# A fused attention and mixture-of-experts kernel: token halves and eight placing transfers, unused rows zeroed by VectorE, a reordered start and two changes at the gates

## The chip, the cores and the metric

The kernel runs on one NeuronCore of a Trainium2 chip. The metric is the device time of one execution in microseconds, from three runs, of which the median counts. The engines are named as the profile names them: PE is TensorE (matmul; PEld its weight load), DVE is VectorE, ACT is ScalarE, POOL is GpSimd, SP is SyncE, which only issues DMA transfers; ACTq is the queue of transfers that ACT issues.

## What is computed

Four batches of eight heads of masked attention over 768 tokens of 64 numbers, and then a layer of eight experts of which each token takes its two best. A pair of tokens is masked out unless q and k have the same nearest of 16 centroids.

```python
q_assign = np.argmax(np.einsum('bhsd,hcd->bhsc', q_n, c_n), axis=-1)
k_assign = np.argmax(np.einsum('bhsd,hcd->bhsc', k_n, c_n), axis=-1)
mask = q_assign[:, :, :, None] == k_assign[:, :, None, :]
scores = np.where(mask, scale * np.matmul(q, k.transpose(0, 1, 3, 2)), -1e9)
attn = softmax(scores); x = attn @ v            # x: 3072 tokens of 512
noisy_logits = x @ w_gate + np.log1p(np.exp(x @ w_noise)) * noise
# the two best of 8 experts per token, softmax of their two logits as weights
out[mask] += top2_w[mask, k, None] * (np.maximum(x[mask] @ w1[e], 0.0) @ w2[e])
```

## The kernel before

**Attention** runs over 16 pairs of heads, p = 0 to 15, twelve steps to a pair (two heads s of six key chunks kc). A step computes the scores of 128 keys against all 768 queries (`scores`, L540 to L549: two matmuls per half of the queries, one of A and one of B, and exp on ACT), `split_p` takes the low part of the result on POOL (L560), and four steps later `values` multiplies with v (L581 to L587). A and B are operands of 128 rows: the high and low parts of q and k, the cluster mask in rows 64 to 80 of A, the negated maxima in rows 96 and 97 of B. Three of each exist and take turns (p % 3); rows that nothing writes are zeroed, and two rows of ones set, once for each of the three by `fixed_init` (L344 to L346).

**The preparation of a pair** comes some steps ahead: `a_split` transposes q and k (L414, PE), copies the high part (L423, ACT) and subtracts for the low part (L424, DVE), into the tile hl (xt for p = 1); `b_place` moves these by DMA into A and B (L488); `a_sims` and `a_sum` (L435, L450) give the similarities with the centroids; five operations on DVE make one-hot rows of them, the mask chain (L454, L458, L462, L467, L471); `a_mask` transposes these (L480) and copies them (L482, ACT, tile mk), `b_mask` moves them into A. `b_max` computes the plain q times k in high parts (L517) and reduces it to row maxima (L520, DVE, 24 reductions per pair), `b_neg` (L527 to L529) and `b_negT` (L534, L536, a DMA) put the negated maxima into B. For p = 0 the last three run for each head alone, before its scores.

**The order** is written out by hand: `attention` (from L200) gives each piece of work a place `at(step, function)` in steps and thirds of steps, from the table AT and some formulas; negative places run before the first score. Each engine executes its instructions in the order in which the code then writes them, waiting for what they need. SP's and ACT's transfers are issued in order as well. PSUM results go to a ring of six banks (`ps()`), and one further bank, aux, is shared by half of the maxima of `b_max` and the gate's small results.

**The gate** (`g_gate`) runs once per batch, three times among the steps and the last time in the experts' beginning, as a list of small pieces that `chain` and `emit` write out. Its `places` multiplies the chosen experts with a triangle and with ones (L780, L784) to count each token's place in its expert's list; L799 and L801 read the counts; L812, L813, L817, L818 and L827 (DVE) and L814 (ACT) pack the results for the lists.

**The experts** go through tokens in tiles: layer 1 (L1271), layer 2 (L1309). w2 is split into high (L1155, ACT) and low parts (L1157, DVE), four quarters, by `split_w2(e, c)`; `eff` issues layer 2 of a tile. For the first expert the quarters are split between pieces of the last gate.

Of the kernel before, what the change touches and what calls it, by code (L numbers as in the profile page):

```python
# [34 lines left out]
    vd=[1, 1, 2, 3, 4, 5], sec=-6.0, qf=-4.0, place1=0.0,  # L35
    fv=[{'v': -5.0, 'vscale': 13.0, 'am': 24.333, 'amstep': 0.333, 'vsplit': 25.333, 'vstep': 2.0},
        {'v': 9.0, 'vscale': 11.667, 'am': 13.333, 'amstep': 0.333, 'vsplit': 15.0, 'vstep': 1.667}],
# [7 lines left out]
class Kernel:  # L45
# [154 lines left out]
    def attention(self, ctx):  # L200
# [6 lines left out]
        self.fix = fix = ctx.enter_context(tc.tile_pool(name="fix", bufs=1))  # L207
        self.A = [fix.tile([128, 2, 2, S], F32R, name=f"A{i}") for i in range(3)]
        self.Bt = [fix.tile([128, 2, 2, S], F32R, name=f"B{i}") for i in range(3)]
        self.oh = [fix.tile([128, 2, 3, 4, 32], BF, name=f"oh{i}") for i in range(2)]  # L210
# [17 lines left out]
        for p in range(NP):  # L228
# [178 lines left out]
    def a_split(self, p, i, s):  # L407

        nc = self.nc
        b, hp = divmod(p, self.H // 2)  # L410
        qk = self.qk[b, hp // 2]
        t = self.ps()[:, :384]
        for m in range(3):
            nc.tensor.transpose(t[:, m * 128:m * 128 + 128],  # L414
                                qk[:, i, 2 * (hp % 2) + s, 2 * m:2 * m + 2, :].rearrange("p j d -> p (j d)"),
                                self.ident)
        if (i, s) == (0, 0):

# [3 lines left out]
        hi, lo = hl[:, 1 + i, s], hl[:, 3 - 3 * i, s]  # L422
        nc.scalar.activation(hi, t, AF.Copy)  # L423
        nc.vector.tensor_tensor(lo, t, hi, op=OP.subtract)  # L424

    def a_sims(self, p, s):

        nc, st = self.nc, self.st[p]
        hp = p % (self.H // 2)
        t = self.ps()[:, :384]  # L430
        n = 0
        for i in range(2):
            c0 = 64 - 64 * i
# [68 lines left out]
    def b_mask(self, p):
        mk, A = self.st[p]["mk"], self.A[p % 3]
        for i in range(2):
            for a in range(2):
                self.dma(A[64:80, i, :, 384 * a:384 * a + 384], mk[64 * i + 32 * a:64 * i + 32 * a + 16],
                         self.nc.scalar if p < 3 and a else None)

    def b_max(self, p, s, j):

        nc, st, A = self.nc, self.st[p], self.A[p % 3]
        if (s, j) == (0, 0):
            st["mm"] = self.wk.tile([128, 2 * self.NJ], F32, name="mm")
        c = self.NJ * s + j
        for n in range(2):
            t = self.ps()[:, :384]
            nc.tensor.matmul(t, A[:, 0, s, j * 128:j * 128 + 128],  # L517
                             A[:, 1, s, n * 384:n * 384 + 384], start=True, stop=True)
            o = st["mm"][:, c:c + 1] if n else self.aux[:, 500 + c:501 + c]
            nc.vector.tensor_reduce(o, t, axis=X, op=OP.max, negate=True)  # L520

    def b_neg(self, p, s, n):

        v, W, c = self.nc.vector, n * self.NJ, self.NJ * s
        o = self.aux[:, 500 + c:500 + c + W]
        hi, lo = (self.nm[:, W * i:W * i + W] for i in range(2))
        v.tensor_tensor(o, o, self.st[p]["mm"][:, c:c + W], op=OP.min)  # L527
        v.tensor_copy(hi, o)
        v.tensor_tensor(lo, o, hi, op=OP.subtract)  # L529

    def b_negT(self, p, s, n):
# [4 lines left out]
        nc.scalar.activation(nt[:W], t[:W, :128], AF.Copy)  # L536
        self.dma(self.Bt[p % 3][96:98, 1, s:s + n], nt[:W], nc.scalar if p < 2 else None)


    def scores(self, p, s, kc):  # L540
        nc, st, A, Bt = self.nc, self.st[p], self.A[p % 3], self.Bt[p % 3]
        ks = slice(kc * 128, kc * 128 + 128)
        pe = self.wk.tile([128, 2, 384], F32, name="pe", bufs=6)
        for n in range(2):
            t = self.ps()[:, :384]
            ns = slice(n * 384, n * 384 + 384)
            for M, qi in ((A, 0), (Bt, 1)):
                nc.tensor.matmul(t, M[:, 1 - qi, s, ks], M[:, qi, s, ns], start=not qi, stop=bool(qi))  # L548
            nc.scalar.activation(pe[:, n], t, AF.Exp, bias=self.l64[:, 0:1], scale=self.scale)  # L549
# [168 lines left out]
    def g_gate(self, b):  # L718
# [183 lines left out]
    def experts(self, ctx):  # L902
# [31 lines left out]
        for f in range(NF):  # L934
# [434 lines left out]
```

## Time and profile before

| | |
|---|---|
| three runs | 1053.3, 1053.99, 1056.56 us; median 1053.99 |
| the profiled execution | 1051.78 us, span 1050.0 us from the first to the last instruction |
| PE busy | 993.1 us, 95% of the span |
| DVE, POOL, ACT busy | 662.6, 575.7, 509.5 us |
| mean granted clock of PE | 0.987 of full speed |

All rows below come from the one profiled execution. An engine's order of time lists start, duration, line and operation, out<-in and the count of alike ones in a row, and in brackets how long the engine had been idle and what released it. "Busy" of a stretch is the sum for each engine in it, in the order PE, PEld, DVE, ACT, POOL, and then come PEclk, the share of the DMA engines and GB/s; PEclk is the clock granted to PE as a share of full speed (1.00 is 2.4 GHz, 0.50 is 1.2 GHz).

### The profile page before, as it was taken

The numbers are of one execution on the slowest core, as the hardware profiler recorded it, in microseconds if no ns is written. First come the engines' busy times: TensorE is split into PE (matmuls) and PEld (weight loads), VectorE is DVE, ScalarE is ACT, GpSimd is POOL, SyncE is SP. The second block draws the span as 40 slices with busy tenths as digits, with TensorE's granted clock in tenths as the row PEclk, the third lists the DMA queues.
The fourth block names the chain that finished last, engine by engine and source line by source line (L and its number), as shares of the span: only waits on it lengthen the run. The fifth ranks groups of instructions, "written<-read, shape, count | busy, mean of one in ns | idle before, by whom it ended". The sixth has DMA issues, their size and how long they took to land.

```text
span 1050.0 us, 21873 instructions
## 1 busy us (share of the span) xinstructions
PE 993.1 (95%) x8353; PEld 672.8 (64%) x8353; DVE 662.6 (63%) x1443; ACT 509.5 (49%) x1059; POOL 575.7 (55%) x631
## 2 busy tenths in 40 slices
PE   5789999999999999899999999999999999999994
PEld 4678998988888888784555545455454454554541
DVE  4787777787778777996646556545555455445421
ACT  3468776767686767577243416234153151421510
POOL 9168786868997799882355225242252442523211
PEclk9699999999999999999999999999999999999997
DMA  7866978787878766317396928729259297391201
GB/s 190 210 168 137 223 175 208 172 202 165 209 181 194 172 148 148 125 53 172 112 210 167 218 95 190 188 85 250 92 143 220 74 189 179 105 235 69 61 34 35
DMA packets 172879, 162.79 MB, mean 155 GB/s; under 512 B 87737, under 2 KB 151609, under 8 KB 172770
## 3 DMA queue, kind: packets, MB, share of 16 engines
q1 hardware_dynamic: 159132, 124.65, 50.6%
q0 software_dynamic: 13296, 36.38, 12.3%
q8 instruction: 67, 1.10, 0.4%
q10 hardware_dynamic: 342, 0.32, 0.2%
q14 instruction: 42, 0.34, 0.1%
HBM read 78.21 MB, written 26.51 MB: 100 GB/s over the span
## 4 chain that ended last, share of the span: by engine, by line
PE 41%; issue 7%; POOL 2%; DMA 2%; ACT 1%; DVE 1%; SPq 0%; POOLq 0%; ACTq 0%
PE ring L1271 20%; PE ring L1309 18%; POOL out L1321 1%; PE ring L1299 1%; DMA xT<-xg 1%; POOL xt L1284 1%; PE ring L1302 0%; PE ring L1176 0%; DMA xg<-xs,idx 0%; DMA xs<-xh 0%; PE ring L692 0%; POOL xh L652 0%; SPq L1262 0%; DMA out<-yo,idx 0%; PE ring L700 0%
## 5 line engine op out<-in xcount | busy, mean ns | idle before, releaser
L560 POOL TENSOR_TENSOR pl<-pe 128x768 f16<-128x768 f32 x173 | 252.0, 1471 | 63.1 <-ACT pe L549 51.7
L1271 PE MATMUL ring<-xT,w1t 128*128 128x416 f16 (+2 forms) x1536 | 272.8, 339 | 0.5 <-DMA xT<-xg 0.5
L1309 PE MATMUL ring<-w2t,hT 128*128 128x512 f16 x1152 | 252.5, 379 | 0.6 <-ACT w2t L1155 0.5
L549 ACT ACTIVATE pe<-ring,l 128x384 f32<-128x384 f32 x384 | 201.1, 578 | 66.9 <-PE ring L548 61.6
L1271 PEld LDWEIGHTS <-w1t 128*128 128x128 f16 x1536 | 149.3, 98 | 119.2 <-issue 1.6
L1309 PEld LDWEIGHTS <-hT 128*128 128x128 f16 x1152 | 112.1, 98 | 134.2 <-issue 1.5
L1148 ACT ACTIVATE hr<-ring 128x416 f32<-128x416 f32 (+2 forms) x128 | 66.5, 519 | 271.1 <-PE ring L1271 271.1
L1321 POOL DMA_INDIRECT out<-yo,idx x52 | 62.3, 1199 | 223.5 <-DVE yo L1317 109.9
L520 DVE TENSOR_REDUCE aux<-ring 128x1 f32<-128x384 f32 x192 | 107.8, 562 | 65.0 <-PE ring L517 56.5
L548 PE MATMUL ring<-A 128*128 128x384 f32 x384 | 143.2, 373 | 1.7 <-ACT mk L482 0.7
L548 PE MATMUL ring<-B 128*128 128x384 f32 x384 | 129.5, 337 | 0.0
L1151 DVE TENSOR_TENSOR hT<-hr,hT 128x416 f16<-128x416 f32 (+3 forms) x128 | 70.6, 557 | 81.5 <-ACT hT L1150 81.3
L517 PE MATMUL ring<-A 128*128 128x384 f32 x384 | 109.2, 359 | 10.3 <-ACT pe L549 3.4
L1317 DVE SCALAR_TENSOR_TENSOR yo<-ring,we,xt 128x512 f32<-128x512 f32 (+1 forms) x49 | 36.7, 748 | 121.0 <-PE ring L1309 106.9
L520 DVE TENSOR_REDUCE mm<-ring 128x1 f32<-128x384 f32 x192 | 105.0, 547 | 0.5 <-PE ring L517 0.5
L1251 POOL DMA_INDIRECT xg<-xs,idx x52 | 57.3, 1102 | 83.1 <-DMA xT<-xg 73.5
L581 PE MATMUL av<-vv,pe 128*128 128x65 f16 x1152 | 97.1, 195 | 0.4 <-DVE stg L595 0.2
L583 PE MATMUL av<-vv,pe 128*128 128x64 f16 x1152 | 96.2, 192 | 0.0
L581 PEld LDWEIGHTS <-pe 128*128 128x128 bf16 x1152 | 79.4, 99 | 15.2 <-issue 10.2
L517 PEld LDWEIGHTS ring<-A 128*128 128x128 f32 x384 | 71.3, 193 | 23.0 <-ACT pe L549 12.5
L583 PEld LDWEIGHTS <-pe 128*128 128x128 bf16 x1152 | 77.8, 98 | 0.3
L548 PEld LDWEIGHTS ring<-A 128*128 128x128 f32 x384 | 73.1, 190 | 6.5 <-ACT pe L549 2.0
(224 smaller groups left out, 1383.3 us busy)
## 6 DMA issues: line engine op xcount, KB each, us to landing
stg<-in_moe_w SPq DMA_DIRECT2D x64, 512.0 KB
A<-hl SPq DMA_DIRECT2D x30, 384.0 KB
B<-hl SPq DMA_DIRECT2D x30, 384.0 KB
vt<-in_v SPq DMA_DIRECT2D x8, 768.0 KB
out<-zt SPq DMA_DIRECT2D x12, 512.0 KB
A<-hl SPq DMA_DIRECT2D x60, 96.0 KB
B<-hl SPq DMA_DIRECT2D x30, 192.0 KB
xs<-xh SPq DMA_DIRECT2D x15, 384.0 KB
```

The source lines that it names most:

```text
L517: nc.tensor.matmul(t, A[:, 0, s, j * 128:j * 128 + 128], A[:, 1, s, n * 384:n * 384 + 384], start=True, stop=True)
L520: nc.vector.tensor_reduce(o, t, axis=X, op=OP.max, negate=True)
L548: nc.tensor.matmul(t, M[:, 1 - qi, s, ks], M[:, qi, s, ns], start=not qi, stop=bool(qi))
L549: nc.scalar.activation(pe[:, n], t, AF.Exp, bias=self.l64[:, 0:1], scale=self.scale)
L560: (nc.vector if last else nc.gpsimd).tensor_tensor(lo, pe, hi, op=OP.subtract)
L581: nc.tensor.matmul(av[:, j, :], ph[:, js], vv[:, hh, kj, 64:129], start=(kc == 0 and j == 0), stop=False, skip_group_check=True)
L583: nc.tensor.matmul(av[:, j, :64], ph[:, js], vv[:, hh, kj, 0:64], start=False, stop=False, skip_group_check=True)
L1148: nc.scalar.activation(r[:, :n], p, AF.Relu, scale=2.0 ** -HT)
L1151: nc.vector.tensor_tensor(h1, r[:, a:b], h0, op=OP.subtract)
L1271: nc.tensor.matmul(p, self.w1t[:, wi, c, f * 128:f * 128 + 128], self.xT[e][:, c, xi, n0:n1], start=(i == 0), stop=(i == 3 * ND - 1))
L1309: nc.tensor.matmul(p, self.hT[:, hi, f, t * 128:t * 128 + 128], self.w2t[:, wi, f], start=(i == 0), stop=(i == 3 * NF - 1))
L1321: i = nc.gpsimd.indirect_dma_start(out=self.out, out_offset=bass.IndirectOffsetOnAxis(ap=en[:r], axis=0), in_=yo[:r], in_offset=None, boun ...
```

## The change

1. **Layout and placing.** A and B, [128, 2, 2, 768] before (part, head, token), become [128, 2, 2, 2, 384] (part, half of the tokens, head, token), and in hl the low part of i stands at slot 3i. `b_place` needs eight transfers for a pair in place of ten, with pieces of 768 numbers instead of 384 and the same bytes; the matmuls keep shapes and number. For p = 0 the negated maxima of a head go out in two transfers instead of one.
2. **Zeroing.** `fixed_init` runs on DVE instead of POOL, at other places.
3. **Third pair sooner, v later.** `a_split` of p = 2 goes to steps -15 and -13, its `b_place` to -11; the load of the first v goes from step -5 to -0.333.
4. **Gates.** The counts of `places` go to a bank of the ring instead of aux, in all four gates.
5. **Last gate.** Its last pieces come ahead of `split_w2(0, 3)` instead of behind `eff(0, 0, TA)`.

```diff
-    fv=[{'v': -5.0, 'vscale': 13.0, ...
+    fv=[{'v': -0.333, 'vscale': 13.0, ...
...
-        self.A = [fix.tile([128, 2, 2, S], F32R, name=f"A{i}") for i in range(3)]
+        self.A = [fix.tile([128, 2, 2, 2, S // 2], F32R, name=f"A{i}") for i in range(3)]
...
-                at(w + P["split"][i], self.a_split, p, i // 2, i % 2)
+                at(w + P["split"][i] if p != 2 else (-15, -13)[i // 2], self.a_split, p, i // 2, i % 2)
...
-            at(w + P["place"] + (T["place1"] if p == 1 else 0), self.b_place, p)
+            at(w + P["place"] + (T["place1"] if p == 1 else 0) if p != 2 else -11, self.b_place, p)
...
-        self.fixed_init(0)
-        at(-14.4, self.fixed_init, 1)
-        at(-8.4, self.fixed_init, 2)
+        at(-26.667, self.fixed_init, 0)
+        at(-25, self.fixed_init, 1)
+        at(-11.333, self.fixed_init, 2)
...
-        nc.gpsimd.memset(self.A[i][64:96].bitcast(F32), 0.0)
-        nc.gpsimd.memset(self.Bt[i][96:128].bitcast(F32), 0.0)
-        nc.gpsimd.memset(self.Bt[i][96:98, 0].bitcast(F32), 1.0)
+        nc.vector.memset(self.A[i][64:96].bitcast(F32), 0.0)
+        nc.vector.memset(self.Bt[i][96:128].bitcast(F32), 0.0)
+        nc.vector.memset(self.Bt[i][96:98, 1].bitcast(F32), 1.0)
...
-            self.dma(A[0:64, :, :, cs], hl[r:r + 64, 1:3])
-            self.dma(A[96:128, 0, :, cs], hl[r:r + 32, 3])
-            self.dma(A[96:128, 1, :, cs], hl[r:r + 32, 2])
-            self.dma(Bt[0:64, :, :, cs], hl[r:r + 64, 0:2])
-            self.dma(Bt[64:96, :, :, cs], hl[r + 32:r + 64, 2:4])
+            self.dma(A[0:64, :, a], hl[r:r + 64, 1:3])
+            self.dma(A[96:128, :, a], hl[r:r + 32, 0:3:2])
+            self.dma(Bt[0:64, :, a], hl[r:r + 64, 1:4:2])
+            self.dma(Bt[64:96, :, a], hl[r + 32:r + 64, 0:3:2])
...
-        self.dma(self.Bt[p % 3][96:98, 1, s:s + n], nt[:W], nc.scalar if p < 2 else None)
+        Bt, by = self.Bt[p % 3], nc.scalar if p < 2 else None
+        if n == 2:
+            self.dma(Bt[96:98, 0], nt[:W], by)
+        else:
+            for a in range(2):
+                self.dma(Bt[96:98, 0, a, s], nt[6 * a:6 * a + 6], by)
...
-        pt = lambda: T["p"][:, 3 * NE:3 * NE + NE + E]
+        pt = lambda: T["pt"][:, :NE + E]
...
         def places():
+            T["pt"] = self.ps()
...
         self.split_w2(0, 2)
+        emit(n3 + 12, len(fs))
         self.split_w2(0, 3)
         self.eff(0, 0, self.TA)
-        emit(n3 + 12, len(fs))
```

How the instructions stand, at three places. Line numbers of the changed kernel differ by a few: L423 is the low part L424, L453 to L470 the mask chain, L516 the reduction L520, L413 the transpose L414, L514 the matmul L517, L479 the transpose L480, L553 the score, L1161 and L1163 the parts of w2, L818 to L833 the gate's end. A_152, A_153 and A_154 are A of the pairs 0, 1 and 2.

DVE in the start, from the last operation on the centroids' weights (wh) to the first maxima; before:

```order
L198 TENSOR_TENSOR wh<-ring,wh 64x8x16 x2
L454 TENSOR_REDUCE mx<-ring 128x24
L458 TENSOR_TENSOR ring<-ring,mx 128x384
L462 TENSOR_TENSOR ring<-ring,revc 128x384
L467 TENSOR_REDUCE km<-ring 128x24
L471 TENSOR_TENSOR oh_158<-ring,km 128x24x16
L424 TENSOR_TENSOR xt<-ring,xt 128x384 x4
```

and now:

```order
L198 TENSOR_TENSOR wh<-ring,wh 64x8x16 x2
L344 MEMSET A_152 32x3072
L345 MEMSET B_155 32x3072
L346 MEMSET B_155 2x1536
L453 TENSOR_REDUCE mx<-ring 128x24
L457 TENSOR_TENSOR ring<-ring,mx 128x384
L461 TENSOR_TENSOR ring<-ring,revc 128x384
L466 TENSOR_REDUCE km<-ring 128x24
L470 TENSOR_TENSOR oh_158<-ring,km 128x24x16
L344 MEMSET A_153 32x3072
L345 MEMSET B_156 32x3072
L346 MEMSET B_156 2x1536
```

The memsets of pair 0 stand ahead of its mask chain, those of pair 1 behind it and ahead of L423 for xt.

DVE from the end of pair 1's mask chain to the first reduction for head 1 of pair 0, now (before, L373 for v stood first and the low parts x4 behind it, with nothing else between):

```order
L470 TENSOR_TENSOR oh_159<-ring,km 128x24x16
L423 TENSOR_TENSOR hl<-ring,hl 128x384 x2
L344 MEMSET A_154 32x3072
L345 MEMSET B_157 32x3072
L346 MEMSET B_157 2x1536
L372 TENSOR_REDUCE vm<-vt 128x2 x2
L516 TENSOR_REDUCE aux<-ring 128x1
```

Half of the third pair's low parts have moved ahead of pair 1's mask chain, half stand before its own memsets.

ACT at the first expert's layer 2, with the last two quarters of w2; before:

```order
L1150 ACTIVATE hT<-ring 128x512
L1155 ACTIVATE w2t<-stg,sw_9581 128x1024 x2
L814 ACTIVATE rec<-aux,px 128x6
L1148 ACTIVATE hr<-ring 128x320
L1150 ACTIVATE hT<-ring 128x256
```

and now:

```order
L1156 ACTIVATE hT<-ring 128x512
L1161 ACTIVATE w2t<-stg,sw_9555 128x1024
L820 ACTIVATE rec<-aux,px 128x6
L1161 ACTIVATE w2t<-stg,sw_9555 128x1024
L1154 ACTIVATE hr<-ring 128x320
```

The gate's operation has moved between the third and the fourth quarter. On DVE likewise:

```order
L1163 SCALAR_TENSOR_TENSOR w2t<-stg,sw_9555,w2t 128x1024
L818 TENSOR_SCALAR aux<-aux 128x12
L819 TENSOR_SCALAR pk<-aux 128x12
L823 TENSOR_TENSOR pk<-aux,pk 128x12
L824 SCALAR_TENSOR_TENSOR rec<-aux,px,gm 128x6
L833 TENSOR_TENSOR lg<-pk,upper 128x672
L1163 SCALAR_TENSOR_TENSOR w2t<-stg,sw_9555,w2t 128x1024
```

The five operations stood behind the fourth quarter before and stand between it and the third now.

## Rows read from the trace of the kernel before

**Rows 1.** Busy time by stretch: length, busy us of each engine (instructions), clock, DMA

```profile
70.00:470.00 400.00, 380.12 (x4960) 343.08 (x4959) 318.80 (x814) 283.89 (x585) 332.88 (x311) 1.00 0.71 168
...
550.00:965.00 415.00, 414.75 (x2163) 208.94 (x2162) 224.37 (x359) 137.08 (x288) 155.39 (x212) 1.00 0.63 158
```

**Rows 2.** TensorE up to the first score: start us, us, instruction [idle <-releaser]

```profile
24.85 1.45 PE L517 MATMUL ring<-A 128*128 128x384 f32 x4 [0.70 <-DMA A<-mk]
...
44.36 0.52 PE L548 MATMUL ring<-A 128*128 128x384 f32 x1
```

**Rows 3.** VectorE's order of time in the start, columns as above

```profile
9.73 0.29 DVE L198 TENSOR_TENSOR wh<-ring,wh 64x128 fp32r<-64x128 f32 x1 [0.34 <-ACT wh L197]
...
15.57 0.56 DVE L454 TENSOR_REDUCE mx<-ring 128x24 f32<-128x384 f32 x1 [5.54 <-PE ring L450]
...
22.64 1.95 DVE L424 TENSOR_TENSOR xt<-ring,xt 128x384 fp32r<-128x384 f32 x4 [4.05 <-ACT xt L423]
...
25.38 0.57 DVE L520 TENSOR_REDUCE aux<-ring 128x1 f32<-128x384 f32 x1 [0.79 <-PE ring L517]
...
31.55 0.17 DVE L529 TENSOR_TENSOR nm<-aux,nm 128x6 fp32r<-128x6 f32 x1
...
33.41 0.56 DVE L454 TENSOR_REDUCE mx<-ring 128x24 f32<-128x384 f32 x1 [1.70 <-PE ring L450]
...
36.27 1.80 DVE L373 TENSOR_REDUCE vm<-vt 128x2 bf16<-128x768 f32 x2
...
40.70 1.95 DVE L424 TENSOR_TENSOR hl<-ring,hl 128x384 fp32r<-128x384 f32 x4 [2.63 <-ACT hl L423]
...
43.00 0.57 DVE L520 TENSOR_REDUCE aux<-ring 128x1 f32<-128x384 f32 x1 [0.35 <-PE ring L517]
```

**Rows 4.** Memsets in the start by form: count | busy us, mean ns | idle before

```profile
L96 DVE MEMSET fw<- 4x128 f32 x1 | 0.2, 165 | 0.0
...
L127 DVE MEMSET l<- 128x1 f32 x1 | 0.1, 59 | 0.0
...
L344 POOL MEMSET A<- 32x3072 f32 x3 | 8.0, 2652 | 0.2
...
L346 POOL MEMSET B<- 2x1536 f32 x3 | 4.1, 1373 | 0.2
```

**Rows 5.** VectorE's order of time, three memsets in a row

```profile
3.49 0.17 DVE L88 MEMSET ones<- 128x128 bf16 x1
3.63 0.17 DVE L90 MEMSET vones<- 128x128 bf16 x1
3.74 0.06 DVE L92 MEMSET tiny<- 128x4 bf16 x1
```

**Rows 6.** Busy time by stretch, as rows 1: the granted clock is behind POOL

```profile
25.00:30.00 5.00, 5.00 (x22) 4.71 (x22) 4.62 (x10) 0.49 (x1) 1.06 (x2) 0.66 0.91 280
...
44.30:46.00 1.70, 1.59 (x8) 1.25 (x7) 1.58 (x4) 0.76 (x2) 0.00 (x0) 0.64 0.53 108
```

**Rows 7.** Order of time around 62 to 68 us, ScalarE's queue and TensorE

```profile
62.29 2.18 ACTq L488 DMA_DIRECT2D A<-mk  x2
...
67.71 0.71 PE L517 MATMUL ring<-A 128*128 128x384 f32 x2 [1.42 <-DVE hl L424]
```

**Rows 8.** TensorE's waits from 70 to 470 us: us in total, times, longest

```profile
PE aux L780 <- DVE aux L520: 3.3, 3, 1.1
...
PE ring L517 <- DMA A<-mk: 0.6, 1, 0.6
```

**Rows 9.** Order of time at layer 2 of the first expert, three engines

```profile
505.36 2.19 ACT L1155 ACTIVATE w2t<-stg,sw 128x1024 f16<-128x1024 f32 x2
506.54 2.48 DVE L1157 SCALAR_TENSOR_TENSOR w2t<-stg,sw,w2t 128x1024 f16<-128x1024 f32 x2 [0.34 <-ACT w2t L1155]
506.56 8.97 PE L1309 MATMUL ring<-w2t,hT 128*128 128x512 f16 x40 [0.54 <-ACT w2t L1155]
...
509.48 0.27 ACT L814 ACTIVATE rec<-aux,px 128x6 f32<-128x6 f32 x1 [1.93 <-DVE pk L813]
```

More of the change, by code (lines that the diff above doesn't have):

```diff
@@ L35 @@
     vd=[1, 1, 2, 3, 4, 5], sec=-6.0, qf=-4.0, place1=0.0,
-    fv=[{'v': -5.0, 'vscale': 13.0, 'am': 24.333, 'amstep': 0.333, 'vsplit': 25.333, 'vstep': 2.0},
+    fv=[{'v': -0.333, 'vscale': 13.0, 'am': 24.333, 'amstep': 0.333, 'vsplit': 25.333, 'vstep': 2.0},
         {'v': 9.0, 'vscale': 11.667, 'am': 13.333, 'amstep': 0.333, 'vsplit': 15.0, 'vstep': 1.667}],
@@ L207, in attention @@
         self.fix = fix = ctx.enter_context(tc.tile_pool(name="fix", bufs=1))
-        self.A = [fix.tile([128, 2, 2, S], F32R, name=f"A{i}") for i in range(3)]
-        self.Bt = [fix.tile([128, 2, 2, S], F32R, name=f"B{i}") for i in range(3)]
+        self.A = [fix.tile([128, 2, 2, 2, S // 2], F32R, name=f"A{i}") for i in range(3)]
+        self.Bt = [fix.tile([128, 2, 2, 2, S // 2], F32R, name=f"B{i}") for i in range(3)]
         self.oh = [fix.tile([128, 2, 3, 4, 32], BF, name=f"oh{i}") for i in range(2)]
@@ L421, in a_split @@
         hl = self.st[p]["hl"]
-        hi, lo = hl[:, 1 + i, s], hl[:, 3 - 3 * i, s]
+        hi, lo = hl[:, 1 + i, s], hl[:, 3 * i, s]
         nc.scalar.activation(hi, t, AF.Copy)
@@ L434, in a_sims @@
             for part in range(2):
-                nc.tensor.matmul(t, self.wh[:, 2 * hp + s, c0:c0 + 128], st["hl"][:, (3 - 3 * i) if part else 1 + i, s, :],
+                nc.tensor.matmul(t, self.wh[:, 2 * hp + s, c0:c0 + 128], st["hl"][:, 3 * i if part else 1 + i, s, :],
                                  start=(n == 0), stop=(n == 3))
@@ L493, in b_place @@
             r = 64 * a
-            cs = slice(384 * a, 384 * a + 384)
-            self.dma(A[0:64, :, :, cs], hl[r:r + 64, 1:3])
-            self.dma(A[96:128, 0, :, cs], hl[r:r + 32, 3])
-            self.dma(A[96:128, 1, :, cs], hl[r:r + 32, 2])
-            self.dma(Bt[0:64, :, :, cs], hl[r:r + 64, 0:2])
-            self.dma(Bt[64:96, :, :, cs], hl[r + 32:r + 64, 2:4])
+            self.dma(A[0:64, :, a], hl[r:r + 64, 1:3])
+            self.dma(A[96:128, :, a], hl[r:r + 32, 0:3:2])
+            self.dma(Bt[0:64, :, a], hl[r:r + 64, 1:4:2])
+            self.dma(Bt[64:96, :, a], hl[r + 32:r + 64, 0:3:2])
     def b_mask(self, p):
@@ L505, in b_mask @@
             for a in range(2):
-                self.dma(A[64:80, i, :, 384 * a:384 * a + 384], mk[64 * i + 32 * a:64 * i + 32 * a + 16],
+                self.dma(A[64:80, i, a], mk[64 * i + 32 * a:64 * i + 32 * a + 16],
                          self.nc.scalar if p < 3 and a else None)
@@ L513, in b_max @@
             st["mm"] = self.wk.tile([128, 2 * self.NJ], F32, name="mm")
-        c = self.NJ * s + j
+        a, m = divmod(j, 3)
+        c = 6 * a + 3 * s + m if p else self.NJ * s + j
         for n in range(2):
             t = self.ps()[:, :384]
-            nc.tensor.matmul(t, A[:, 0, s, j * 128:j * 128 + 128],
-                             A[:, 1, s, n * 384:n * 384 + 384], start=True, stop=True)
+            nc.tensor.matmul(t, A[:, 0, a, s, m * 128:m * 128 + 128], A[:, 1, n, s], start=True, stop=True)
             o = st["mm"][:, c:c + 1] if n else self.aux[:, 500 + c:501 + c]
@@ L525, in b_neg @@
         o = self.aux[:, 500 + c:500 + c + W]
-        hi, lo = (self.nm[:, W * i:W * i + W] for i in range(2))
+        nm = self.nm[:, :2 * W]
+        hi, lo = (nm.rearrange("p (a r m) -> p a r m", a=2, m=3)[:, :, i] if n == 1 else nm[:, W * i:W * i + W]
+                  for i in range(2))
         v.tensor_tensor(o, o, self.st[p]["mm"][:, c:c + W], op=OP.min)
+        if n == 1:
+            o = o.rearrange("p (a m) -> p a m", m=3)
         v.tensor_copy(hi, o)
@@ L536, in b_negT @@
         nc.scalar.activation(nt[:W], t[:W, :128], AF.Copy)
-        self.dma(self.Bt[p % 3][96:98, 1, s:s + n], nt[:W], nc.scalar if p < 2 else None)
+        Bt, by = self.Bt[p % 3], nc.scalar if p < 2 else None
[4 more added lines that the diff above has]
+                self.dma(Bt[96:98, 0, a, s], nt[6 * a:6 * a + 6], by)
     def scores(self, p, s, kc):
         nc, st, A, Bt = self.nc, self.st[p], self.A[p % 3], self.Bt[p % 3]
-        ks = slice(kc * 128, kc * 128 + 128)
+        a, m = divmod(kc, 3)
+        ks = slice(m * 128, m * 128 + 128)
         pe = self.wk.tile([128, 2, 384], F32, name="pe", bufs=6)
@@ L545, in scores @@
             t = self.ps()[:, :384]
-            ns = slice(n * 384, n * 384 + 384)
-            for M, qi in ((A, 0), (Bt, 1)):
-                nc.tensor.matmul(t, M[:, 1 - qi, s, ks], M[:, qi, s, ns], start=not qi, stop=bool(qi))
+            for i, M in enumerate((A, Bt)):
+                nc.tensor.matmul(t, M[:, 1, a, s, ks], M[:, 0, n, s], start=not i, stop=bool(i))
             nc.scalar.activation(pe[:, n], t, AF.Exp, bias=self.l64[:, 0:1], scale=self.scale)
```

## Prediction, made before the changed kernel ran

> **What bounds the kernel now.** I read the busy time by stretch first. Between 70 and 470 us TensorE (PE) works 380.12 of 400 us, and between 550 and 965 us 414.75 of 415 [rows 1]. So nothing there is to be had except PE's own waits, and a delay of the work that feeds PE for the first time goes straight to the end. The second view is PE's start: its first score matmul (L548) begins at 44.36 us, and the one-head maxima before it (L517) began at 24.85 us, released by the mask's transfer into A [rows 2]. Third, I followed VectorE (DVE) through the start [rows 3]. It is the engine that the change loads, and it has three holes there: 5.54 us before the first mask chain (L454 at 15.57), 4.05 us before the second pair's low parts (L424 at 22.64), and 2.63 us before the third pair's low parts (40.70). Last come the places where PE waits later: around 62 to 68 us, at the gates' counts (L780), and at layer 2 of the first expert.
>
> **Part 1, zeroing on DVE.** The nine memsets of the unused rows leave GpSimd (POOL) and enter DVE's queue: per pair two of 32x3072 and one of 2x1536, that is 7680 elements along a partition. On POOL the large one takes 2652 ns and the small one 1373 ns [rows 4], together 6.68 us. DVE has no such large memset in the trace, so its price is bounded. From 1 to 128 elements its row grows from 59 to 165 ns [rows 4], 0.835 ns an element, 6.4 us for 7680. By the starts of memsets in a row, 3.49, 3.63 and 3.74 us [rows 5], 128 elements hold the engine 0.11 to 0.14 us, 0.86 to 1.09 ns an element, 6.6 to 8.4 us. I take 6.8 us a pair (0.885 ns), near the rows' slope and POOL's 6.68, and keep 6.4 and 8.4. A price far below the 6.4 isn't excluded by a row of that length; it is a rival.
>
> On this point the Trainium skill, page "VectorE: DVE Perf Modes", section "Zero memsets can be issued as uint32 (trn2)", says that a memset takes one cycle per element whatever the type. The trace agrees that the type makes no difference: L88 in 2-byte elements [rows 5] has a row as long as L96 in 4-byte ones [rows 4]. With the page's 0.96 GHz an estimate is 8.0 us a pair; the sum by it would be 3.6 us higher than mine.
>
> Now DVE's queue in its new order, everything by starts in [rows 3]. The last wh operation ends at 9.73 + 0.29 = 10.02. Pair 0's memsets follow, to 16.8; the hole of 5.54 us swallows most of it. The mask chain takes 36.27 - 33.41 = 2.86 us (the second one, up to the next operation's start), to 19.7. Pair 1's memsets stand between it and the second pair's low parts: to 26.5, where that operation began at 22.64 before. Its four take 1.95: 28.4. The twelve reductions of head 0 and the negation take 31.72 - 25.38 = 6.34 (L529 begins at 31.55 and takes 0.17): 34.75. The mask chain of pair 1 began 33.41 - 31.72 = 1.69 after that, since PE has to transpose the negated maxima (L534) and to sum the similarities (L450) first. The third pair's two low parts (half of 1.95) fit into these 1.69 us, and its six transposes on PE stand before L534, in time that PE waits anyway: 36.45. Mask chain: 39.3. Two more low parts: 40.3. Pair 2's memsets: 47.1. The maxima of v (L373), 1.80: 48.9. Only then comes the first maximum of head 1, which was at 43.00.
>
> The first score needs the PSUM bank that this reduction (0.57 us) frees: 49.5 against 44.36, **+5.15 us**. In general the shift is 5.15 + 3 x (m - 6.8), m being the price of a pair: +4.0 at 6.4 and +10 at 8.4. The mask's transfer, which released L517 at 24.85 before, has 3.5 us more to land and isn't last any more.
>
> Then PE begins its scores cold. Where it took up work after a pause before, the granted clock was below full: 0.66 from 25 to 30 us, 0.64 from 44.3 to 46 [rows 6], so part of those stretches ran at the lower of the two levels (1.2 and 2.4 GHz). Now it will have stood for about 5 us ahead of the scores, and loses somewhat more than before. I add 0.5 us, 0 to 1.
>
> **Part 2, third pair sooner, v later.** The third pair's placing can leave earlier against the scores, and the loads of q and k behind it on SyncE (SP) with it. Before, ScalarE (ACT) was held 2.18 us at 62.29 issuing the third pair's mask transfers, behind those loads; the exp after it came late, the next high parts too, and PE waited 1.42 us for the low part at 67.71 [rows 7]. With the loads gone out before the scores are far on, this wait goes: -1.7 us with the smaller gaps beside it, between 0 and -2.3. Moving the v load behind the next q and k on SP costs nothing: its first reader, L373, comes at 48.9 instead of 36.27 [rows 3].
>
> **Part 3, eight placing transfers.** Bytes stay, pieces double in length, two issues per pair go. PE waits for a transfer into A only 0.6 us in 70 to 470 [rows 8], so 0 to -0.6; I take 0. The matmuls keep their number and shapes. For pair 0 the transposed maxima go out in two transfers on ACT's queue instead of one; the second, up to 1.2 us, lies beside DVE's longer chain. If that cover went it would cost its length.
>
> **Part 4, gates' places in the ring.** PE waited 3.3 us in three places for the auxiliary bank, which the running maxima write too [rows 8]. In the ring the counts wait for a maximum some four reductions earlier, long done. The ring lends a bank until DVE has added the counts (L799, L801), so a later allocation comes nearer to its reader: I take -2.3, between 0 and -3.3.
>
> **Part 5, the last gate's end before the last quarter of w2.** On ACT, L814 now stands between the third and the fourth high part (L1155), and it waits for DVE's L813, which stands behind DVE's third low part (L1157). Before, the last two high parts ran 505.36 to 507.55 and the low ones 506.54 to 509.02, and PE took the fourth as it came [rows 9]. L814 followed 0.46 us after the last low part, at 509.48. Now the third low part ends at 506.54 + 1.24 = 507.8, so L814 begins at 508.2 and takes 0.27, and the fourth high part runs 508.5 to 509.6. PE, with nothing else in its order than layer 2 (forty matmuls without a gap from 506.56 [rows 9]), stops for 509.6 - 507.55 = **2.0 us**, between 0 and 2.2. POOL's routing work that becomes earlier isn't on PE's path.
>
> **The sum**: 5.15 + 0.5 - 1.7 + 0 - 2.3 + 2.0 = +3.65 us. Against the profiled execution, 1051.78 us with a span of 1050.0, that is 1055.4. The median of the three runs shown, 1053.99, lies 2.2 above it; on the median: **1057.6 us**. A measurement of this kernel can tell about 0.3%, 3.2 us: faster is below 1050.8, slower above 1057.2.
>
> **Rivals.**
> *Full price* (chance 0.20): 128 elements in 0.14 us, the longer of the two distances in [rows 5]. Then m is about 8, the shift 8.75, the time 1061.2. For it speaks that distance, against it the other one and the slope of the rows. The page named above asks for nearly this.
> *Cheap memset, faster* (0.17): DVE writes two elements where POOL writes one, m about 3.3. Pair 0's lie in the 5.54 us hole, pair 1's end at about 21.9, ahead of 22.64, and pair 2's begin at 37.2 and end at 40.5; the first maximum of head 1 comes at 42.3, the first score at 42.9, -1.5. The sum is -1.5 - 1.7 - 2.3 + 2.0 = -3.5: 1050.5, and 1049 with the gates' whole 3.3. It decides from m = 5.1 downwards, where the shift is nothing. Against it: no memset row of the trace goes faster than 0.835 ns an element.
> *The start doesn't hang on DVE* (0.13): if the placing transfers stay last (L517's releaser at 24.85 was one [rows 2]), the memsets lie under them, the start stays, and -1.7 - 2.3 + 2.0 gives 1052.0. Against it: pair 0's transfers have no v load ahead of them now, and pair 2's memsets stand behind everything that could wait for one.
> *The last gate costs nothing* (0.06): were L813 done early the 2.0 us fall away: 1055.6. The wait stands in the order.
> *My forecast* with m from 6.4 to 7.4: 1056 to 1060 (0.44).
>
> **How the numbers follow.** Slower: the full price and six tenths of the forecast's case, 0.46. Same: the rest of that case, the last gate, and most of the third, 0.32. Faster: the cheap memset and some of the third, 0.22. The range reaches from the cheap memset, 1049.5, to 8.4 us a pair with part of the gains, 1063.5.
>
> **What would show it.** Right: DVE's large memset rows of 2.6 to 2.9 us (bounds 2.6 to 3.4), the second at 22 to 27 us ahead of L424; first score at 49 to 51 us; no ACT queue row of 2 us near 62 us plus the shift; no PE wait at the gates' L780; a PE wait of 2 us at L1309 near 510, released by ACT's L1155. Wrong: memset rows under 1.7 us; a first score before 45 us; PE waiting at the ring for the gates' DVE rows by as much as it waited at the auxiliary bank.

## The result, and the profile after

The changed kernel takes 1067.54 us, the median of four runs (1066.46 to 1068.37); the kernel before took 1055.28 in four runs beside it. The ratio is 1.0111, 95% interval 1.0092 to 1.013: slower by 1.1%, some 12 us, where 0.34% slower had been forecast, and outside the range. The profiled execution of the changed kernel spans 1064.7 us, that of before 1050.0.

VectorE's order of time in the start of the changed kernel, the columns as in [rows 3]:

```profile
9.40 0.29 DVE L198 TENSOR_TENSOR wh<-ring,wh 64x128 fp32r<-64x128 f32 x1 [0.34 <-ACT wh L197]
...
10.27 2.62 DVE L344 MEMSET A<- 32x3072 f32 x1 [0.58 <-issue]
13.59 2.62 DVE L345 MEMSET B<- 32x3072 f32 x1 [0.70 <-issue]
16.59 1.34 DVE L346 MEMSET B<- 2x1536 f32 x1 [0.38 <-DVE B L345]
17.96 0.56 DVE L453 TENSOR_REDUCE mx<-ring 128x24 f32<-128x384 f32 x1
...
20.42 0.56 DVE L470 TENSOR_TENSOR oh<-ring,km 128x384 bf16<-128x384 f32 x1
21.67 2.62 DVE L344 MEMSET A<- 32x3072 f32 x1 [0.69 <-issue]
...
29.35 1.95 DVE L423 TENSOR_TENSOR xt<-ring,xt 128x384 fp32r<-128x384 f32 x4
...
41.99 1.01 DVE L423 TENSOR_TENSOR hl<-ring,hl 128x384 fp32r<-128x384 f32 x2
43.69 2.62 DVE L344 MEMSET A<- 32x3072 f32 x1 [0.69 <-issue]
...
51.35 1.81 DVE L372 TENSOR_REDUCE vm<-vt 128x2 bf16<-128x768 f32 x2
53.08 0.56 DVE L516 TENSOR_REDUCE aux<-ring 128x1 f32<-128x384 f32 x1
```

A large memset has a row of 2.62 us, as expected, but the next one doesn't begin when the row ends: 13.59 - 10.27 = 3.32 us lie between two starts, and the last wh operation had ended at 9.69. From there to the mask chain at 17.96 pair 0's zeroing takes 8.27 us. Pair 1's goes from 20.98 to 29.35, pair 2's from 43.00 to 51.35: 8.37 and 8.35 us. The first reduction for head 1 comes at 53.08 instead of 43.00 [rows 3], and TensorE's first score behind it:

```profile
53.69 0.69 PE L553 MATMUL ring<-A 128*128 128x384 f32 x1 [6.94 <-DVE aux L516]
```

It was at 44.36 [rows 2]: 9.33 us later. TensorE's busy time and clock by stretch there, ahead of the first score and with the first scores (columns as in [rows 1]):

```profile
49.00:53.60 4.60, 0.00 (x0) 0.00 (x0) 4.21 (x6) 0.00 (x0) 0.00 (x0) 0.50 0.94 186
53.70:57.30 3.60, 3.60 (x12) 3.29 (x13) 3.38 (x9) 1.53 (x3) 1.25 (x1) 0.50 0.96 230
```

The lower of the two levels holds for the first 3.6 us of the scores, where before it was 0.64 of full over 1.7 us [rows 6]. Half of 3.6, less 0.36 of 1.7, makes some 1.2 us more lost than before. Further on, ScalarE's and TensorE's order of time at the third pair's mask:

```profile
72.55 1.47 ACTq L487 DMA_DIRECT2D A<-mk  x2
74.12 1.05 ACT L554 ACTIVATE pe<-ring,l 128x384 f32<-128x384 f32 x2 [1.60 <-PE ring L413]
...
77.26 0.70 PE L514 MATMUL ring<-A 128*128 128x384 f32 x2 [1.37 <-DVE hl L423]
```

The wait of 1.42 us at 67.71 [rows 7] is still there, 1.37 us. One line of TensorE's waits from 70 to 470 us, before and then in the changed kernel:

```profile
PE ring L480 <- DVE oh L471: 1.9, 4, 0.6
```

```profile
PE ring L479 <- DVE oh L470: 3.5, 6, 1.0
```

No wait for the gates' counts is left in that view (it was 3.3 us [rows 8]), but this one, the transposing of the masks' one-hot rows, has grown; experiment 7 says by how much for the gates' sake. Last, layer 2 of the first expert in three engines, as in [rows 9]:

```profile
515.80 1.28 DVE L1163 SCALAR_TENSOR_TENSOR w2t<-stg,sw,w2t 128x1024 f16<-128x1024 f32 x1 [0.35 <-ACT w2t L1161]
515.81 1.02 PE L1315 MATMUL ring<-w2t,hT 128*128 128x512 f16 x4 [0.54 <-ACT w2t L1161]
517.20 0.17 DVE L819 TENSOR_SCALAR pk<-aux 128x12 int32<-128x12 int32 x1
517.41 0.27 ACT L820 ACTIVATE rec<-aux,px 128x6 f32<-128x6 f32 x1 [1.65 <-DVE pk L819]
517.57 1.14 ACT L1161 ACTIVATE w2t<-stg,sw 128x1024 f16<-128x1024 f32 x1
518.76 9.43 PE L1315 MATMUL ring<-w2t,hT 128*128 128x512 f16 x36 [1.92 <-ACT w2t L1161]
```

TensorE stops for 1.92 us for the fourth high part, which waits for L820, which waits for L819 behind the third low part: the chain of the prediction. What it didn't have is the clock behind the stop, by stretch:

```profile
518.80:521.00 2.20, 2.20 (x6) 0.80 (x6) 1.37 (x2) 0.00 (x0) 0.00 (x0) 0.50 0.00 0
521.00:523.00 2.00, 2.00 (x9) 0.78 (x7) 0.00 (x0) 0.00 (x0) 0.00 (x0) 0.79 0.00 0
```

PEclk is 0.50 for 2.2 us and 0.79 for another 2, and then full. And the second expert's first transfer is waited for longer, 0.23 us before (order of time) and 2.0 now (waits from 500 to 550 us):

```profile
528.78 3.42 PE L1271 MATMUL ring<-xT,w1t 128*128 128x320 f16 x24 [0.23 <-DMA xT<-xg]
```

```profile
PE ring L1277 <- DMA xT<-xg: 2.0, 1, 2.0
```

### The profile page after: what moved, and what is told of

Read it like the earlier page. It is cut to its first block, busy times and chain, and to the rows that moved or that the text cites. A ratio compares the mean times of both kernels' runs of the same rounds, so it can differ in the third digit from the quotient of the medians.

```text
span 1064.7 us, 21837 instructions
## 1 busy us (share of the span) xinstructions
PE 993.4 (93%) x8353; PEld 671.8 (63%) x8353; DVE 681.7 (64%) x1452; ACT 508.8 (48%) x1059; POOL 554.4 (52%) x622
## 4 chain that ended last, share of the span: by engine, by line
PE 41%; issue 7%; POOL 2%; DMA 2%; ACT 1%; DVE 1%; SPq 0%; POOLq 0%; ACTq 0%; DVEq 0%
PE ring L1277 20%; PE ring L1315 18%; DMA xT<-xg 1%; POOL out L1327 1%; PE ring L1305 1%; POOL xt L1290 1%; PE ring L1308 0%; PE ring L1182 0%; DMA xg<-xs,idx 0%; DMA xs<-xh 0%; PE ring L697 0%; POOL xh L657 0%; SPq L1268 0%; DMA out<-yo,idx 0%; PE ring L705 0%
## 5 line engine op out<-in xcount | busy, mean ns | idle before, releaser
L553 PE MATMUL ring<-A 128*128 128x384 f32 x384 | 144.1, 375 | 8.8 <-DVE aux L516 7.6
L516 DVE TENSOR_REDUCE aux<-ring 128x1 f32<-128x384 f32 x192 | 107.9, 562 | 60.9 <-PE ring L514 50.8
L553 PE MATMUL ring<-B 128*128 128x384 f32 x384 | 130.0, 339 | 0.2 <-issue 0.2
L514 PE MATMUL ring<-A 128*128 128x384 f32 x384 | 109.3, 360 | 9.2 <-ACT pe L554 4.3
L516 DVE TENSOR_REDUCE mm<-ring 128x1 f32<-128x384 f32 x192 | 105.2, 548 | 0.0
L514 PEld LDWEIGHTS ring<-A 128*128 128x128 f32 x384 | 71.9, 195 | 22.3 <-ACT pe L554 12.2
L553 PEld LDWEIGHTS ring<-A 128*128 128x128 f32 x384 | 73.3, 191 | 15.0 <-DVE aux L516 9.1
```

The costliest lines, as they stand in the source:

```text
L514: nc.tensor.matmul(t, A[:, 0, a, s, m * 128:m * 128 + 128], A[:, 1, n, s], start=True, stop=True)
L553: nc.tensor.matmul(t, M[:, 1, a, s, ks], M[:, 0, n, s], start=not i, stop=bool(i))
```

## Experiments

Each is compared with the kernel before in runs on the same chip; the level of both moves by some 5 us between sets of runs, so ratios are what counts. "First score" is the start of the first matmul of `scores` in the profiled execution.

**1. The zeroing back on GpSimd, all else changed.**

```diff
-        at(-26.667, self.fixed_init, 0)
-        at(-25, self.fixed_init, 1)
-        at(-11.333, self.fixed_init, 2)
+        self.fixed_init(0)
+        at(-14.4, self.fixed_init, 1)
+        at(-8.4, self.fixed_init, 2)
...
-        nc.vector.memset(self.A[i][64:96].bitcast(F32), 0.0)
+        nc.gpsimd.memset(self.A[i][64:96].bitcast(F32), 0.0)
```

> The changed kernel with the zeroing of the unused rows back on GpSimd at its old places; all else stays changed. Theory A (the memsets hold VectorE 8.2 us a pair, and the start hangs on VectorE): the first score, at 53.69 us in the changed kernel and 44.36 before, comes at 41 to 44.5 us, and the time falls by 10 to 13 us from 1067.5, to 1054.5 to 1057.5. Rival B (the start's delay is mostly taken back by later waits, and the loss sits in the later changes): the first score comes as early as in A, but the time falls by less than 5 us, to 1063 or more.

Ratio 0.9999 (0.9978 to 1.0019), against 1.0111 for the whole change: moving the zeroing is worth 1.1%, nearly 12 us, the whole of the loss. The first score comes at 40.84 us, as early as theory A wanted and a little more:

```profile
40.84 0.34 PE L553 MATMUL ring<-A 128*128 128x384 f32 x1
```

Rival B is out: what the start loses is not taken back.

**2. The zeroing on VectorE alone, added to the kernel before.**

```diff
-        self.fixed_init(0)
-        at(-14.4, self.fixed_init, 1)
-        at(-8.4, self.fixed_init, 2)
+        at(-26.667, self.fixed_init, 0)
+        at(-25, self.fixed_init, 1)
+        at(-11.333, self.fixed_init, 2)
...
-        nc.gpsimd.memset(self.A[i][64:96].bitcast(F32), 0.0)
+        nc.vector.memset(self.A[i][64:96].bitcast(F32), 0.0)
```

> The kernel before with one edit: the zeroing on VectorE at the places of the change. Theory A: pair 0's memsets end near 18 us, pair 1's near 29.5, pair 2's stand ahead of the maxima of v and the third pair's four low parts; the first score comes at 55 to 56 us, 11 us later than before, plus 1 us for the lower clock at the scores' beginning: 1066 to 1068. Rival B (the third pair's earlier preparation is what delays the start): the first score before 50 us and 1060 or less.

Ratio 1.0106 (1.0075 to 1.0136), 11 us. The first score is at 56.69, a little behind theory A's 55 to 56 and later still than in the whole change, since the third pair's four low parts now stand behind its memsets too:

```profile
49.96 1.34 DVE L346 MEMSET B<- 2x1536 f32 x1 [0.38 <-DVE B L345]
...
53.04 1.94 DVE L424 TENSOR_TENSOR hl<-ring,hl 128x384 fp32r<-128x384 f32 x4
...
56.69 0.53 PE L548 MATMUL ring<-A 128*128 128x384 f32 x1
```

Taken away from the change or added to the kernel before, the same edit gives the same 11 to 12 us. It moves the memsets to another engine and to other places in the order at once; VectorE at other places wasn't run.

**3. The last gate's end back behind layer 2's first tile, all else changed.**

```diff
-        emit(n3 + 12, len(fs))
         self.split_w2(0, 3)
         self.eff(0, 0, self.TA)
+        emit(n3 + 12, len(fs))
```

> The changed kernel with the last gate's end back behind layer 2's first tile. Theory A (TensorE's stop of 1.92 us ahead of the fourth quarter of w2 lets its clock fall, and the two together cost 3.4 us): no wait at L1315 for the fourth high part above 0.6 us, granted clock 1.00 in the 8 us behind it, the time 3.4 us lower, near 1064; and 1.7 us more, 1062.4, if the later wait of 2.0 us for the second expert's gather goes as well. Rival B (the wait of 1.92 us alone counts): 1065.6.

Ratio 1.01 (1.0069 to 1.0132), against 1.0111: about 1 us, with intervals that overlap widely. In its trace the wait is 0.5 us and the granted clock 1.00 behind it, as A wants, and the wait for the gather 0.4; but the median went down by less than either theory said, and the intervals hold both. Experiments 4 and 11 say more.

**4. Both back.** The edits of 1 and 3 together.

> The changed kernel with both undone, the zeroing on GpSimd and the last gate's end behind layer 2's first tile: what is left is the layout, the third pair sooner, the later v load and the gates' counts in the ring. Theory A (the two losses add up): 1050 to 1053, that is 2 to 5 us under the kernel before. Rival B (what is left gains nothing, since a wait that goes comes back at the next one): 1054 to 1057, the same as before.

Ratio 0.9968 (0.9952 to 0.9984): faster than the kernel before by 0.3%, as by A. Against the first experiment, which ran beside it, moving the gate's end back is worth 0.31%, 3.3 us by the medians, though the two intervals still touch (0.9978 to 1.0019 there). In its trace the stop of 1.92 us is gone, but TensorE waits 2.39 us for the second expert's gather, and its granted clock is 0.50 over the 3.35 us behind that.

**5. What a VectorE memset costs.** Eight memsets ahead of pair 0's, on rows that are written over later.

```diff
+        at(-26.667, self.price)
         at(-26.667, self.fixed_init, 0)
...
+    def price(self):
+        v, A, Bt = self.nc.vector, self.A[2], self.Bt[2]
+        for M in (A, Bt):
+            v.memset(M[0:32].bitcast(F32), 0.0)
+        for M in (A, Bt):
+            v.memset(M[32:64, 0].bitcast(F32), 0.0)
+        for M in (A, Bt):
+            v.memset(M[32:64, 1, 0].bitcast(F32), 0.0)
+        for M in (A, Bt):
+            v.memset(M[32:64, 1, 1, 0].bitcast(F32), 0.0)
```

> The changed kernel with eight more VectorE memsets ahead of pair 0's, on rows of the third pair's A and B that the placing overwrites later: two each of 32x3072, 32x1536, 32x768 and 32x384, none over another's rows, GpSimd idle. Theory A (the engine is held about 1.05 ns an element and the row shows only part of it): starts follow one another after 3.2 to 3.3, 1.6 to 1.7, 0.80 to 0.85 and 0.40 to 0.45 us. Rival B (the row is right at 0.85 ns an element, and each memset waits about 0.7 us for its issue, whatever its length): 3.3, 2.0, 1.35 and 1.0 us. By A the first score comes 12.5 us later than in the changed kernel, by B 15.3.

VectorE's order of time:

```profile
10.21 2.62 DVE L346 MEMSET A<- 32x3072 f32 x1 [0.69 <-issue]
13.42 2.62 DVE L346 MEMSET B<- 32x3072 f32 x1 [0.59 <-issue]
16.39 1.34 DVE L348 MEMSET A<- 32x1536 f32 x1 [0.36 <-issue]
18.00 1.34 DVE L348 MEMSET B<- 32x1536 f32 x1 [0.27 <-issue]
19.44 0.70 DVE L350 MEMSET A<- 32x768 f32 x1
20.25 0.70 DVE L350 MEMSET B<- 32x768 f32 x1
20.98 0.38 DVE L352 MEMSET A<- 32x384 f32 x1
21.39 0.38 DVE L352 MEMSET B<- 32x384 f32 x1
22.44 2.62 DVE L356 MEMSET A<- 32x3072 f32 x1 [0.68 <-issue]
```

Between two memsets of the same length the starts are 3.21, 1.61, 0.81 and 0.41 us apart. That halves with the length, as A says: 1.05 to 1.07 ns an element, while the rows of the long ones say 0.85. A constant wait at the issue (B) would have left over 1 us between the shortest ones. What the row lacks lies ahead of it and goes with the memset's own length: 0.6 to 0.7 us ahead of 3072 elements, 0.3 to 0.4 ahead of 1536, 0.1 ahead of 768. The last row above shows it best: it starts 1.05 us after one of only 384 elements, which holds the engine 0.41 us when one of its own length follows. So the "idle" that the view puts down to issue is part of the memset. The first score is at 66.19 us, 12.5 later than in the changed kernel, as by A.

**6. The layout alone.** The kernel before with A and B by token halves, eight placing transfers and the slots that go with them; the core of it is the part of the diff above from the tiles' shapes to `b_negT`.

```diff
-            self.dma(A[0:64, :, :, cs], hl[r:r + 64, 1:3])
+            self.dma(A[0:64, :, a], hl[r:r + 64, 1:3])
...
-            self.dma(A[96:128, 0, :, cs], hl[r:r + 32, 3])
-            self.dma(A[96:128, 1, :, cs], hl[r:r + 32, 2])
+            self.dma(A[96:128, :, a], hl[r:r + 32, 0:3:2])
```

> The kernel before with the layout by token halves alone (eight placing transfers, the negated maxima of pair 0 in two). Theory A (TensorE hardly waits for these transfers): ratio 0.999 to 1.001, first score within 0.7 us of 44.36. Rival B (the placing paces the start): first score at 43 us or sooner, ratio 0.998 or less.

Ratio 1.0006 (0.9992 to 1.002), as by A for the time. The first score of its profiled execution is at 41.89 us, 2.5 earlier than before, which is what B said of the start; but no time came of it, and in experiments 7 and 11, which change nothing there, it is at 43.29 and 43.45. With the third pair sooner it is at 39.97 and 39.23 in the old layout (experiments 8 and 10) and at 40.84, 39.71 and 40.61 in the new one (1, 4 and 9). That the layout makes the start shorter is not shown.

**7. The gates' counts in the ring alone.**

```diff
-        pt = lambda: T["p"][:, 3 * NE:3 * NE + NE + E]
+        pt = lambda: T["pt"][:, :NE + E]
...
         def places():
+            T["pt"] = self.ps()
```

> The kernel before with the gates' counts in a ring bank alone. Theory A (the three waits of 1.1 us go, but what is won at the third comes back before the last pair's negated maxima, and 0.3 to 0.4 us at each of the others at the next reductions): 1.4 us less, ratio 0.998 to 0.9995. Rival B (all 3.3 us stay won): ratio 0.997 or less. Rival C (the lent bank costs as much as it brings): 0.9995 to 1.0005, with TensorE waits at the ring behind the gates.

Ratio 0.9987 (0.9976 to 0.9999): 1.4 us, as by A, with an interval from 0.1 to 2.5. Part of what is won comes back at the next transposes of one-hot rows, right behind the first two gates, 0.32 and 0.33 us where the kernel before has no wait; TensorE's order of time behind the first:

```profile
223.58 0.51 PE L480 MATMUL ring<-identb,oh 128*128 128x128 bf16 x6 [0.32 <-DVE oh L471]
```

VectorE is as far as it was; TensorE comes to the next thing that it wants of it sooner. Every kernel with the ring bank has six waits at this line, every kernel without it four. The rest of the growth from 1.9 to 3.5 us at this line is not the ring's: the two waits of 0.5 us at 252.9 and 363.0 before are 0.98 here, but 0.98 too in experiments 6, 8 and 11, which have no ring bank. At the third gate the traces don't settle what comes back: the wait for the negated maxima (L534) ahead of it is 1.30 us here and nothing before, but the other kernels without the bank have anything from nothing to 1.3 there too.

**8. The third pair sooner and v later alone.**

```diff
-    fv=[{'v': -5.0, 'vscale': 13.0, ...
+    fv=[{'v': -0.333, 'vscale': 13.0, ...
...
-                at(w + P["split"][i], self.a_split, p, i // 2, i % 2)
+                at(w + P["split"][i] if p != 2 else (-15, -13)[i // 2], self.a_split, p, i // 2, i % 2)
...
-            at(w + P["place"] + (T["place1"] if p == 1 else 0), self.b_place, p)
+            at(w + P["place"] + (T["place1"] if p == 1 else 0) if p != 2 else -11, self.b_place, p)
```

> The kernel before with the third pair's split and placing sooner and the first v later, zeroing on GpSimd. Theory A (the third pair's transposes and low parts leave the way to the first score, the wait near 65 us stays): first score at 40.5 to 41.5 us, ratio 0.9965 to 0.998. Rival B (the wait of 1.42 us behind ScalarE's mask transfers goes too): ratio 0.9955 or less. Rival C (the start's gain comes back until 70 us): ratio 0.999 or more.

Ratio 0.9979 (0.9965 to 0.9992), 2.2 us, as by A. The first score, which A had at 40.5 to 41.5, is 4.4 us earlier than in the trace of before and 3.3 earlier than in experiment 7; not all of that reaches the end. First score and the wait that stayed:

```profile
39.97 0.52 PE L548 MATMUL ring<-A 128*128 128x384 f32 x1
...
PE ring L517 <- DVE hl L424: 1.4, 1, 1.4
```

**9. Experiment 4 with the third pair's mask transfers off ScalarE's queue.**

```diff
-                         self.nc.scalar if p < 3 and a else None)
+                         self.nc.scalar if p < 2 and a else None)
```

> The kernel of the fourth experiment (zeroing on GpSimd, last gate's end back) with one more edit: the third pair's two mask transfers on ScalarE's queue go to SyncE's. Theory A (the wait near 65 us was ScalarE's own issuing of two transfers, 1.2 to 2.2 us with or without loads ahead of them): the exp behind the mask's copy follows at once, TensorE's wait for the third pair's low part, 1.1 to 1.4 us, falls below 0.4, and the ratio goes from 0.9968 to 0.9955 to 0.996. Rival B (the mask arrives later on SyncE and TensorE waits for it instead): the ratio stays at 0.9968 or rises.

Ratio 0.9957 (0.9943 to 0.9972), against 0.9968: where A put it, though the two intervals overlap. The mechanism is plain in the trace. ScalarE's order of time:

```profile
58.19 0.99 ACT L481 ACTIVATE mk<-ring,ms 128x768 fp32r<-128x768 bf16 x1 [0.59 <-PE ring L479]
59.59 1.05 ACT L554 ACTIVATE pe<-ring,l 128x384 f32<-128x384 f32 x2 [0.41 <-PE ring L553]
```

The exp begins 0.41 us behind the mask's copy, and TensorE's wait for the low part is not among the waits of that stretch any more. This is the lowest ratio of the study, 0.43% under the kernel before, though not told apart from experiments 4 and 10.

**10. The ring and the third pair in the old layout.** The edits of 7 and 8 together.

> The kernel before with the gates' ring bank and the third pair sooner, the old layout kept. Theory A (the layout does nothing, the other two add up): ratio 0.9958 to 0.9978, 0.9987 times 0.9979 being 0.9966, the same as the fourth experiment. Rival B (the layout is worth something together with the others): 0.998 or more.

Ratio 0.9967 (0.9953 to 0.9981), as by A: with the layout (experiment 4, on another chip) it was 0.9968. The layout is worth nothing measurable.

**11. The last gate's end alone, added to the kernel before.** The edit of experiment 3 in the other direction.

> The kernel before with one edit: the last gate's end ahead of the last quarter of w2. Theory A (TensorE stops 1.9 us and then works at a lower clock): ratio 1.002 to 1.004, a wait of 1.9 us at L1309 for ScalarE's L1155, and granted clock under 0.8 in the 4 us behind it. Rival B (the stop alone): 1.0018 or less and full clock.

Ratio 1.0011 (1.0001 to 1.0021), 1.2 us, by the median as B, though the interval reaches A's 1.002. The stop is the same as in the whole change, and the granted clock stays up (order of time and stretch):

```profile
508.56 3.61 PE L1309 MATMUL ring<-w2t,hT 128*128 128x512 f16 x16 [1.92 <-ACT w2t L1155]
...
509.00:511.00 2.00, 2.00 (x11) 0.94 (x10) 0.97 (x2) 0.00 (x0) 0.00 (x0) 1.00 0.00 0
```

while in experiment 1 the same stop is followed by the lower level:

```profile
501.69 5.58 PE L1315 MATMUL ring<-w2t,hT 128*128 128x512 f16 x18 [1.92 <-ACT w2t L1161]
...
501.50:504.00 2.50, 2.31 (x6) 0.84 (x6) 1.60 (x3) 0.14 (x1) 0.00 (x0) 0.50 0.00 0
```

Experiment 5, which has the stop too (1.93 us, ending at 531.99), shows 0.55 of full from 532.0 to 535.8. So the stop is in the trace of all four kernels with this order, and the lower level behind it, some 1.5 us, in three of them, each seen in one execution. What decides it wasn't settled. That this accounts for the 3.3 us of experiment 1 against 4 and the 1.2 us here is not shown: the intervals don't tell the two apart, and experiments 4 and 9 have a stretch at the lower level too, behind waits of 2.39 and 1.98 us for the gather.

## Why the prediction was wrong, step by step

**The start on VectorE: mechanism right, price wrong.** The queue was worked out as it then ran: the three groups of memsets stand where they were put, and with the formula of the prediction, 5.15 + 3 x (m - 6.8), the measured 8.27 us a pair gives 9.6; the measured shift is 9.33. The first step that failed is the choice of m, and it is the dearest: 4.2 us of the 8.6 that the sum of +3.65 lacks against the 12.3 of the medians. The bounds were 6.4 and 8.4 us, the upper one from the distance of two starts, 0.14 us for 128 elements [rows 5], and I took 6.8, because it lay near the lengths of the rows and near GpSimd's memset [rows 4]. The length of a long VectorE memset's row is 0.85 ns an element, and the engine is held 1.05 to 1.08 ns (experiment 5, and 3.32 us between two large ones in the changed kernel). Of the two distances in [rows 5] only 0.14 us was a price: there a memset of 128 elements follows one of 128, while at 0.11 us one of 4 elements follows, with next to nothing ahead of its row. The sign that was to show the price right, rows of 2.6 to 2.9 us, came true although the price was wrong: a row's length could not test it. The rival at full price was the right one on this term: 8.75 us there. The Trainium skill, page "VectorE: DVE Perf Modes", section "Zero memsets can be issued as uint32 (trn2)", was nearer than the row too: one cycle an element at 0.96 GHz is 1.04 ns, and the trace comes within 4% of it, by distances of starts and not by lengths of rows. With m at 8.27 the prediction's own sum is 8.1 us, 1062 in its terms and still within its range; the terms that follow took the time out of it.

**The clock at the first scores: too small.** 0.5 us had been added. The lower level held for 3.6 us of work instead of part of 1.7, after 6.94 us without any: some 1.2 us, outside the 0 to 1 that had been allowed.

**The third pair: a gain counted where it wasn't.** The loads behind the placing were to leave earlier and take the wait near 65 us with them; I priced it -1.7 us. The wait stayed, 1.42 us then and 1.37 now. ScalarE's 2.18 us there [rows 7] were for the most part its own issuing of two transfers: the changed kernel still takes 1.47, experiment 11, with the loads where they were before, 1.53, and TensorE waits 1.4 us in both; experiment 9, which takes the two transfers off that queue, removes TensorE's wait. What the third pair's earlier preparation does bring is the start, 2.2 us of time alone (experiment 8). The whole change has it too: its first score is at 53.69, that of the zeroing alone (experiment 2) at 56.69.

**Eight transfers: right.** Nothing was expected of them in the steady part, and alone they bring nothing (experiments 6 and 10).

**The gates: direction right, 2.3 taken, 1.4 measured, with an interval that holds both.** The waits at L780 are gone, all 3.3 us. The prediction's reason for less than the whole, a bank of the ring that comes free later, shows nowhere in the waits; the mask's transposes (L480) behind the first two gates take 0.6 us back, and where the rest goes is open (experiment 7).

**The last gate: the stop was right to 0.1 us** (2.0 predicted, 1.92 measured, by the wait that was named). The clock behind it was not in the sum, a term put at nothing: in the profiled execution 2.2 us at 0.50 and 2 us at 0.79 of full speed, 1.1 + 0.4 = 1.5 us.

**Not foreseen: the second expert's gather.** TensorE waits 2.0 us for xT in the changed kernel and 2.0 to 2.4 in experiments 1, 4 and 9, but 0.4 and 0.6 in experiments 3 and 10 and less than 0.3 in the others. The four with the long wait have the layout, the third pair and the ring bank together; experiments 3 and 5 have these as well and don't have the wait. Its cause is open.

On the whole, in the two profiled executions: the first score comes 9.33 us later, and the first matmul of layer 2 still 9.25 later; what is lost in between (the scores' clock, and the gaps of the last section) and what is gained (the gates) about cancel:

```profile
504.13 1.89 PE L1309 MATMUL ring<-w2t,hT 128*128 128x512 f16 x8
```

```profile
513.38 1.89 PE L1315 MATMUL ring<-w2t,hT 128*128 128x512 f16 x8
```

Behind it come 1.9 us for the stop, 1.5 for its clock and 1.75 more for the gather: 14.4 of the 14.7 us between the two spans. The medians are 12.3 apart. The profiled execution of before, 1051.78, was faster than all four beside the changed kernel, and how many of the others had the last two losses isn't known.

## What to carry to other kernels

Price an instruction that is to stand in a full queue by the distance of starts between two of its kind and of the same length, not by the length of its row: the row of a long VectorE memset hid a fifth of what it holds the engine. Work that an idle engine does for nothing, here 20 us of zeroing on GpSimd, can be dear on the engine whose order leads to the first matmul: VectorE took 25 us for it, and half of that came out as time. And a transfer's issue is an instruction of the queue that it stands in: ask what it holds up there before asking what it waits for.

## What the hardware showed that was not expected

A stop of TensorE of 1.92 or 1.93 us at the same instruction was followed by a stretch at the lower clock in three kernels (the changed one, experiments 1 and 5) and by full clock in a fourth (experiment 11). Stops of 2.39 and 1.98 us for the gather were followed by such a stretch in experiments 4 and 9, and stops of 1.98 and 2.22 us for it were not in the changed kernel and experiment 1.

Between 456 and 470 us of the changed kernel TensorE has gaps that no releaser explains, 1.4 us together, the largest group of them in its waits from 70 to 470 us:

```profile
PE av L588 <- issue: 0.8, 2, 0.4
```

Experiments 5 to 11 have 1.4 to 1.6 us of such gaps at about the same place of the program, the kernel before and experiments 1 to 4 none. Experiments 1 to 4 ran on one chip and 5 to 11 on two others: the gaps go with the chip or the set of runs and not with an edit. Their cause is open.

With the zeroing off GpSimd one VectorE operation of the start has another length. Before, and then in the changed kernel:

```profile
6.07 2.11 DVE L186 TENSOR_SCALAR c<-c,cn 128x128 f32<-128x128 f32 x1
```

```profile
6.07 0.28 DVE L186 TENSOR_SCALAR c<-c,cn 128x128 f32<-128x128 f32 x1
```

It is the same operation of 128x128 elements beside GpSimd's first memset (5.44 to 8.09 us) and without it. All nine kernels with the zeroing on GpSimd have 2.11 or 2.12 us here, the four without 0.28 or 0.29. It doesn't go for every operation: the last wh operation (L198, 0.29 us) and the first of the mask chain (L454, 0.56) are as long beside GpSimd's later memsets as without them. The end of this chain gains 0.33 us, 10.02 against 9.69.
